# A fused attention and expert kernel: the first stage's loads four units ahead and in program order, TensorE's order left to the scheduler

## The chip, the cores and the metric

The kernel runs on one core of one Trainium2 chip. The metric is device time in microseconds (us) of one execution. A core has TensorE (PE, matrix multiplies into PSUM banks), VectorE (DVE), ScalarE (ACT), GpSimd (POOL) and SyncE (SP, which here issues every DMA). Each engine works through its own list of instructions, and that list is fixed when the program is built.

## The reference, cut to what matters

Three blocks follow one another on float32 data:

```
# 1  q, k, v: (4, 8 heads, 576, 64)
out_d     = softmax(q_d @ k_d.T / 8) @ v_d      # q_d, k_d, v_d: means over 4 positions (144 rows)
out_local = softmax(q @ k.T / 8, masked to |i - j| < 4) @ v
x = repeat(out_d, 4) + out_local                # -> (4, 576, 512)
# 2  a token mixer, then a channel mixer
u = x + (relu(x.T @ w_tok1) @ w_tok2).T         # w_tok1 576x256, w_tok2 256x576
x = u + relu(u @ w_ch1) @ w_ch2                 # w_ch1 512x1536, w_ch2 1536x512
# 3  four attention experts with causal masks, each row weighted by its two best gates
```

The weights of block 2 arrive in a 64-bit format and are turned into float32 on the core. They, and the activations that meet them, are split into a high and a low part, so that each product is three matmuls.

## The kernel before, in words

**Units.** The first stage (blocks 1 and the token mixer of 2) loops over 16 units, a batch `b` and a pair of heads `p` each. A unit's data are `qT` (queries, transposed), `kz` (keys, two halves in a zeroed tile), `vz` (values in windows of 64 positions, two halves in a zeroed tile) and `vp` (values for the mean). `load_qk` (L271) loads the first two and `load_v` (L254) the others. `load_v` also adds up `vp` into `vd` on GpSimd (L265, L266).

**Steps.** Step `i` of the loop at L468 does, in program order: `load_qk` of unit `i+3`; `values(i)` (matmuls into `pod` and `ol`, and the sum into `u`); `local(i+2)` and `pooled(i+2)` (scores `sl` and `sd`, `kd`, the maxima `nmx` and `nd`, the exponentials into `P` and `Pd`); `turns(i+1)` (transposes `tl` and `pdt`, copied to `PT` and `PdT` by ScalarE); `tok_step(i)`; four pieces of the token mixer's weights, while there are any; from step 3 on one piece `wc` of the channel mixer's weights, six in all for its first group; and `load_v` of unit `i+3`. `tok_step` (L461) does the token mixer for the pair of units whose last is done: transposes `tx` (`tok_turn`) and then the second product `pu` (`tok_second`) of an older pair in even steps, the first product `h` (`tok_first`) in odd steps.

**Weights.** `load_f32` (L166) loads a 64-bit piece into one of two `raw64` buffers, and ScalarE, VectorE and GpSimd convert it (L190 to L200); `split` then makes its two parts.

**Buffers.** `KB` (3) counts the `kz` and `qz` tiles, `VB` (3) the `vz` tiles and the units that `load_v` is ahead, `LA+1` (3) the units that `load_qk` is ahead. `qT` has 3 buffers, `vp` 2, `vd` 3. `pod`, `ol`, `sd`, `tl`, `tx`, `h` and `pu` share 4 PSUM banks; `sl` and `pdt` share 2 double ones.

**What sets the order.** The framework's scheduler simulates the program when it is built and gives each engine its list: an instruction is put in when the simulation has it ready, the earlier or the favoured one (`PRI`) first. VectorE's, ScalarE's, GpSimd's and SyncE's lists come from this. TensorE's list in the first stage is written out by hand: `behind` (L90) chains each matmul and transpose to the one before in program order, with

```
tc.add_manual_dep(ins.ins, order["last"].ins.name, ...NoSync..., reason="order")
```

SyncE's list isn't chained: a load is issued where the simulation found its buffer free.

After the stage, `order["on"] = False` (L487), and stage two (the channel mixer, L570 on) and the experts follow, whose order is the scheduler's.

Of the kernel before, what the change touches and what calls it, by code (L numbers as in the profile page):

```python
# [7 lines left out]
F32 = mybir.dt.float32  # L8
# [8 lines left out]
B, H, S, D = 4, 8, 576, 64  # L17
# [9 lines left out]
PK, PQ = SD // 2, 2 * SD // 3  # L27
# [18 lines left out]
ZENG = ['any', 'any']  # L46
PRE = False
ABANKS, CBANKS = (4, 2), (6, 1)
START = 'q0 q1 v0 q2 v1 v2'
XLO = 'gpsimd'  # L50
CONV0 = 3
UB = 5
TAIL = [1, 1, 1, 1]
ULO = 'vector'
LA = 2
WT = 4
VB = 3
KB = 3


@with_exitstack
def body(ctx, tc, qT, kT, vw, vp, wt1, wt2, wc1, wc2, wq, wk, wvg, wo, out):
    nc = tc.nc

    def pool(name, side=None, space=None, stack=ctx):
        kw = {"side": side} if side else {}
        if space is not None:
            kw["space"] = space
        return stack.enter_context(tc.tile_pool(name=name, bufs=1, reuse_waits="tile", **kw))
# [13 lines left out]
    def ahead(part):  # L83

        return tc.high_priority(offset=PRI[part]) if part in PRI else nullcontext()

    def spare(kind, i=0):

        return nc.vector if i < VEC.get(kind, 0) else nc.gpsimd

    order = {"on": True, "last": None}

    def behind(ins):

        if order["on"]:
            if order["last"] is not None:
                tc.add_manual_dep(ins.ins, order["last"].ins.name,
                                  mybir.DependencyInfo(mybir.DependencyClass.NoSync, mybir.DependencyReason.DATA),
                                  reason="order")
            order["last"] = ins  # L100

    def mm(*a, **kw):
        behind(nc.tensor.matmul(*a, **kw))  # L103

    def tp(*a):
        behind(nc.tensor.transpose(*a))
# [29 lines left out]
    def split(hi, lo, src, relu=False, scale=None):  # L136
        nc.scalar.activation(hi, src, AF.Relu if relu else AF.Copy, **({"scale": scale} if scale else {}))  # L137
        lowpart(lo, src, hi, relu, scale)
# [18 lines left out]
    def flat(t, shape):  # L157
        return t.rearrange("p c n -> p (c n)") if len(shape) == 3 else t

    def load_split(p, dram, shape, name, stage):  # L160
        raw = stage.tile(shape, F32, tag="raw", bufs=2, name=name + "_raw")
        nc.sync.dma_start(raw, dram)
        hi = p.tile(shape, F32R, name=name + "_hi")
        lo = p.tile(shape, F32R, name=name + "_lo")
        split(hi, lo, raw)
        return hi, lo  # L166

    def load_f32(dram, shape, name, dst=None):

        P0, n = shape[0], 1  # L170
        for d in shape[1:]:
            n *= d
        if dram.dtype == F32:
            if dst is None:
                dst = pv.tile(shape, F32, tag="w64t", bufs=2, name=name + "_t")
            nc.sync.dma_start(dst, dram)
            return dst
        raw = pv.tile([P0, n, 2], I32, tag="raw64", bufs=2, name=name + "_raw")
        d32 = dram.bitcast(I32)
        if len(shape) == 3:  # L180
            nc.sync.dma_start(raw.rearrange("p (c n) t -> p c (n t)", c=shape[1]), d32)
        else:
            nc.sync.dma_start(raw.rearrange("p n t -> p (n t)"), d32)
        h = raw[:, :, 1]
        a = pv.tile([P0, n], I32, tag="w64a", bufs=2, name=name + "_a")
        f = pv.tile([P0, n], I32, tag="w64f", bufs=2, name=name + "_f")
        g = pv.tile([P0, n], F32, tag="w64g", bufs=2, name=name + "_g")
        t = pv.tile([P0, n], F32, tag="w64t", bufs=2, name=name + "_t")

        nc.scalar.activation(t.bitcast(I32), raw.bitcast(U32)[:, :, 0], AF.Copy, scale=2.0 ** -29)  # L190

        nc.scalar.activation(g, h.bitcast(F32), AF.Abs)

        nc.vector.tensor_scalar(a, h, 3, 0x3FFFFFF8, op0=OP.logical_shift_left, op1=OP.bitwise_and)
        nc.vector.scalar_tensor_tensor(f, h, -0x40000000, a, op0=OP.bitwise_and, op1=OP.bitwise_or)
        nc.vector.scalar_tensor_tensor(f.bitcast(F32), g, 2.0 ** -15, f.bitcast(F32), op0=OP.is_ge, op1=OP.mult)
        if dst is None:
            dst = t.rearrange("p (c n) -> p c n", c=shape[1]) if len(shape) == 3 else t

        nc.gpsimd.tensor_tensor(flat(dst, shape).bitcast(I32), f, t.bitcast(I32), op=OP.add)  # L200
        return dst
# [12 lines left out]
    pa = pool("pa", stack=sA)  # L214
# [27 lines left out]

    KZ = [pa.tile([128, 2, S], F32, name=f"kz{i}") for i in range(KB)]
    VZ = [pa.tile([128, 2, NW, D], F32, name=f"vz{i}") for i in range(VB)]

    QZ = [pa.tile([128, 2, SD], F32, name=f"qz{i}") for i in range(KB)]

    def zero(tiles, i, eng):

        for h in range(2):  # L250
            eng.memset(tiles[i][64 * h:64 * h + 64, 1 - h], 0.0)

    Vl, Vd = {}, {}

    def load_v(b, p):
        i = b * NP + p
        if i < VB:
            zero(VZ, i, getattr(nc, ZENG[1]))
        Vl[b, p] = VZ[(b * NP + p) % VB]
        for h in range(2):  # L260
            nc.sync.dma_start(Vl[b, p][64 * h:64 * h + 64, h], vw[b, p, 64 * h:64 * h + 64])
        raw = pa.tile([PK, 4, 4, D], F32, tag="vp", bufs=2, name=f"vp{b}{p}")
        nc.sync.dma_start(raw, vp[b, p])
        vd = pa.tile([PK, 4, D], F32, tag="vd", bufs=3, name=f"vd{b}{p}")
        spare("v", i).tensor_tensor(raw[:, :, 0:2], raw[:, :, 0:2], raw[:, :, 2:4], op=OP.add)  # L265
        spare("w", i).tensor_tensor(vd, raw[:, :, 0], raw[:, :, 1], op=OP.add)  # L266
        Vd[b, p] = vd
# [1 line left out]
    QK = {}  # L269

    def load_qk(b, p):  # L271
        q = pa.tile([128, S], F32, tag="qT", bufs=3, name=f"qT{b}_{p}")
        nc.sync.dma_start(q, qT[b, p])
        i = b * NP + p
        if i < KB:
            zero(KZ, i, getattr(nc, ZENG[0]))
            zero(QZ, i, nc.gpsimd)
        kz = KZ[i % KB]
        for h in range(2):
            nc.sync.dma_start(kz[64 * h:64 * h + 64, h], kT[b, p, 64 * h:64 * h + 64])  # L280
        QK[b, p] = (q, kz, QZ[i % KB])

    SC = {}
# [82 lines left out]
    def values(b, p):  # L366
        PT, PdT = TR.pop((b, p))
        po = b1("pod")
        vd = Vd[b, p]
        for k in range(2):  # L370
            for h in range(2):
                mm(po[64 * h:64 * h + 64, :SD], vd[:, 2 * h + k], PdT[:, k, h * SD:(h + 1) * SD],
                                 start=k == 0, stop=k == 1)
        OdT = pa.tile([128, SD], F32, tag="OdT", bufs=2, name="OdT")
        nc.scalar.activation(OdT, po[:, :SD], AF.Copy)
        up = OdT[:, :, None].to_broadcast([128, SD, 4])
        for w0, w1 in ((0, 4), (4, NW)):
            o = b1("ol")
            s0 = w0 * WQ
            s1 = min(w1 * WQ, S)  # L380
            for w in range(w0, w1):
                q0 = w * WQ
                n = min(WQ, S - q0)
                r0 = 64 * (w % 2) + q0 - KS[w]
                for h in range(2):
                    mm(o[64 * h:64 * h + 64, q0 - s0:q0 - s0 + n], Vl[b, p][:, h, w],
                                     PT[:, w // 2, r0:r0 + n], start=True, stop=True)
            nc.vector.tensor_tensor(U[b][:, p, s0:s1].rearrange("p (g r) -> p g r", r=4),
                                    o[:, :s1 - s0].rearrange("p (g r) -> p g r", r=4),
                                    up[:, s0 // 4:s1 // 4], op=OP.add)  # L390
# [44 lines left out]
    units = [(b, p) for b in range(B) for p in range(NP)]  # L435
    for what in START.split():
        (load_qk if what[0] == "q" else load_v)(*units[int(what[1])])

    n = len(units)
# [20 lines left out]

    def tok_step(i):  # L461

        for what, k in ((tok_turn, i - 2), (tok_first, i - 3), (tok_second, i - 4)):
            if k % 2 == 0 and 0 <= k < n:
                with ahead(what.__name__):
                    what(units[k][0], units[k][1] // 2)

    for i in range(n):  # L468
        if i + LA + 1 < n:
            load_qk(*units[i + LA + 1])  # L470
        values(*units[i])
# [7 lines left out]
        tok_step(i)  # L479
        for _ in range(WT):  # L480
            if tokw:
                tokw.pop(0)()
        if i >= CONV0 and conv[0][0] == 0:
            convert()
        if i + VB < n:
            load_v(*units[i + VB])
    order["on"] = False  # L487
    sA.close()


# [279 lines left out]
    for i, (b, p) in enumerate(pairs):  # L770
# [13 lines left out]
        last = nxt is None  # L784
# [80 lines left out]
```

## Time and profile before

| | |
|---|---|
| time, median of 3 runs | 832.79 us (830.56 to 835.46) |
| time of the profiled execution | 831.15 us |
| its span, first to last instruction | 829.3 us |
| TensorE busy | 696.0 us, 84% of the span |
| VectorE, ScalarE, GpSimd busy | 492.0, 392.2, 163.4 us |
| mean granted TensorE clock | 0.925 of full speed |
| moved by DMA | 46.88 MB |

The profile's page shows the span in 40 slices of some 20.7 us. In the first thirteen, which hold the first stage, TensorE is busy for 4, 4, 2, 4, 4, 6, 8, 5, 6, 8, 5, 8 and 9 tenths, and after them for 9 or more in nearly all. VectorE's for the first six are 5, 5, 9, 8, 9 and 5. A row of the windows view gives, for one stretch, what each engine was busy; a row of the waits view, who waited for whom, in all, how often and at most; a row of the timeline, one instruction or a run of like ones, with the idle time before it and what ended that in brackets. "Busy" leaves out all time in which an engine stands at an instruction that isn't ready.

### The profile page before, as it was taken

Reading aid. Unit: us, or ns where it says so; the run is one execution under the profiler, and the core shown is the slowest. Engines: PE = TensorE matmul, PEld = TensorE weight load, DVE = VectorE, ACT = ScalarE, POOL = GpSimd, SP = SyncE. Lnnn points to the kernel's source line nnn. Section 1 sums busy time; section 2 is a strip of 40 time slices with the busy share of each in tenths; the row PEclk is TensorE's granted clock in tenths of the full one; section 3 lists DMA queues with packets and bytes.
Section 4 is the critical chain, followed back from the end, with each engine's and each line's share of the span. In section 5 each row is a group of like instructions: output and inputs, shape, how many; then the busy total and the mean of one; then the engine's idle time right before and its main releaser. Section 6 shows DMA issues by size and latency. Waiting matters only on the chain. (4 is left out here: it accounts for less than half of the span.)

```text
span 829.3 us, 15409 instructions
## 1 busy us (share of the span) xinstructions
PE 696.0 (84%) x5816; PEld 648.7 (78%) x5816; DVE 492.0 (59%) x1203; ACT 392.2 (47%) x1273; POOL 163.4 (20%) x183
## 2 busy tenths in 40 slices
PE   4424468568589999999999999999989989989994
PEld 3324368557578999999999999999987868779863
DVE  5598955334445479487558445644287556657760
ACT  6356653363365254354344223422266475566662
POOL 5575653333321012020011000000420010010000
PEclk8567598798799999999999999999999999999997
DMA  8545552252210022031011001000021031021111
GB/s 208 141 126 171 157 123 60 60 117 60 59 34 2 1 89 65 2 116 37 1 51 53 1 1 39 15 1 1 1 58 31 1 86 30 9 78 30 44 45 57
DMA packets 28578, 46.88 MB, mean 57 GB/s; under 512 B 3224, under 2 KB 16024, under 8 KB 28504
## 3 DMA queue, kind: packets, MB, share of 16 engines
q1 hardware_dynamic: 28504, 45.90, 20.7%
q8 instruction: 46, 0.75, 0.4%
q14 instruction: 28, 0.23, 0.1%
HBM read 36.45 MB, written 4.72 MB: 50 GB/s over the span
## 5 line engine op out<-in xcount | busy, mean ns | idle before, releaser
L103 PE MATMUL c<-ul,wch 128*128 128x288 f32 x384 | 113.7, 296 | 0.6 <-DVE ul L506 0.6
L103 PE MATMUL c<-uh,wch 128*128 128x288 f32 x384 | 113.6, 296 | 0.4 <-DVE acc L529 0.4
L103 PE MATMUL c<-hh,wch 128*128 128x288 f32 x384 | 113.8, 296 | 0.0
L103 PE MATMUL c<-hh,wcl 128*128 128x288 f32 x384 | 113.2, 295 | 0.0
L103 PE MATMUL c<-hl,wch 128*128 128x288 f32 x384 | 113.2, 295 | 0.0
L103 PE MATMUL c<-uh,wcl 128*128 128x288 f32 x384 | 113.2, 295 | 0.0
L137 ACT ACTIVATE hh<-c 128x288 fp32r<-128x288 f32 x96 | 39.1, 408 | 122.1 <-PE c L103 122.1
L143 DVE SCALAR_TENSOR_TENSOR hl<-c,hh 128x288 fp32r<-128x288 f32 x96 | 43.5, 453 | 64.6 <-ACT hh L137 64.6
L103 PEld LDWEIGHTS c<-ul,wch 128*128 128x128 f32 x384 | 72.4, 189 | 1.5 <-DVE ul L506 1.3
L103 PEld LDWEIGHTS c<-uh,wch 128*128 128x128 f32 x384 | 72.2, 188 | 0.9 <-DVE acc L529 0.9
L103 PEld LDWEIGHTS c<-hh,wch 128*128 128x128 f32 x384 | 72.2, 188 | 0.2
L103 PEld LDWEIGHTS c<-hl,wch 128*128 128x128 f32 x384 | 72.3, 188 | 0.0
L103 PEld LDWEIGHTS c<-hh,wcl 128*128 128x128 f32 x384 | 72.3, 188 | 0.0
L103 PEld LDWEIGHTS c<-uh,wcl 128*128 128x128 f32 x384 | 72.2, 188 | 0.0
L200 POOL TENSOR_TENSOR wc_t<-wc_f,wc_t 128x512 int32<-128x512 int32 x24 | 33.7, 1409 | 171.3 <-ACT wc_t L190 155.3
L505 ACT ACTIVATE uh<-u 128x288 fp32r<-128x288 f32 x128 | 52.9, 441 | 27.3 <-PE c L103 27.3
L506 DVE TENSOR_TENSOR ul<-u,uh 128x288 fp32r<-128x288 f32 x128 | 56.4, 470 | 8.8 <-ACT uh L505 8.7
L700 ACT ACTIVATE Pc<-s,nm 112x576 f32<-112x576 f32 (+4 forms) x80 | 44.3, 555 | 25.6 <-DVE nm L697 13.2
L103 PE MATMUL pod<-PdT,vd 72*64 72x144 f32 x128 | 13.4, 339 | 50.7 <-ACT PdT L363 45.7
L103 PE MATMUL pu<-wt_hi,h1h 128*128 128x288 f32 x64 | 24.0, 375 | 36.4 <-DVE xl L147 35.2
L319 ACT ACTIVATE P<-sl,nmx 128x64 f32<-128x64 f32 x160 | 48.6, 341 | 8.7 <-DVE nmx L313 8.6
L295 DVE TENSOR_REDUCE kd<-kz 128x144 f32<-128x1152 f32 x16 | 21.6, 1348 | 51.3 <-DMA kz<-in_kT_dram 51.3
(166 smaller groups left out, 1880.1 us busy)
## 6 DMA issues: line engine op xcount, KB each, us to landing
wc_raw<-in_wc_dram SPq DMA_DIRECT2D x24, 512.0 KB
vz<-in_vw_dram SPq DMA_DIRECT2D x32, 160.0 KB
qT<-in_qT_dram SPq DMA_DIRECT2D x16, 288.0 KB
kz<-in_kT_dram SPq DMA_DIRECT2D x32, 144.0 KB
vp<-in_vp_dram SPq DMA_DIRECT2D x16, 288.0 KB
K<-K SPq DMA_DIRECT2D x64, 72.0 KB
out_dram<-y SPq DMA_DIRECT2D x16, 232.0 KB
wt_raw<-in_wt_dram SPq DMA_DIRECT2D x4, 288.0 KB
```

The lines of the kernel that those rows point to most:

```text
L103: behind(nc.tensor.matmul(*a, **kw))
L137: nc.scalar.activation(hi, src, AF.Relu if relu else AF.Copy, **({"scale": scale} if scale else {}))
L143: nc.vector.scalar_tensor_tensor(lo, src, 0.0, h, op0=OP.max, op1=OP.subtract)
L200: nc.gpsimd.tensor_tensor(flat(dst, shape).bitcast(I32), f, t.bitcast(I32), op=OP.add)
L295: nc.vector.tensor_reduce(kd, kz.rearrange("p h (g r) -> p g h r", r=4), axis=AX.XY, op=OP.add)
L319: nc.scalar.activation(P[:, t, h], sv[:, bk, i], AF.Exp, bias=nmx[:, bk, i:i + 1], scale=0.125, accum_out=sm[:, t, h:h + 1])
L505: nc.scalar.activation(hi, u, AF.Copy)
L506: getattr(nc, ULO).tensor_tensor(lo, u, hi.bitcast(F32), op=OP.subtract)
L700: nc.scalar.activation(pv_, sv, AF.Exp, bias=nm[:nq], accum_out=su[:nq])
```

## The change

Seven things are changed, all but the last in the first stage.

1. Before the loop the loads go `q0 q1 v0 q2 v1 q3 v2 v3`, one unit more of each; in the loop `load_qk` is of unit `i+4` and `load_v` of `i+4`.
2. There are 4 tiles of `kz`, `qz`, `vz`, `qT` and `vd` instead of 3, and 3 of `vp` instead of 2.
3. All loads of the stage, the weights' too, go through `fetch`, which chains each to the one before: SyncE issues them in program order.
4. `order["on"]` is False: TensorE's list in the stage comes from the scheduler, as the other engines' lists do.
5. In `tok_step` the second product stands ahead of the transposes.
6. Three pieces of the token mixer's weights per step instead of four.
7. The memory that GpSimd's own DMA queue would use is cut to 1024 bytes, which makes room for the tiles.

```diff
-START = 'q0 q1 v0 q2 v1 v2'
+START = 'q0 q1 v0 q2 v1 q3 v2 v3'
-LA = 2
-WT = 4
-VB = 3
-KB = 3
+LA = 3
+WT = 3
+VB = 4
+KB = 4
-    order = {"on": True, "last": None}
+    order = {"on": False, "last": None}
+    queue = {"on": True, "last": None}
+
+    def fetch(dst, src):
+
+        ins = nc.sync.dma_start(dst, src)
+        if queue["on"]:
+            if queue["last"] is not None:
+                tc.add_manual_dep(ins.ins, queue["last"].ins.name,
+                                  mybir.DependencyInfo(mybir.DependencyClass.NoSync, mybir.DependencyReason.DATA),
+                                  reason="queue")
+            queue["last"] = ins
...
-            nc.sync.dma_start(Vl[b, p][64 * h:64 * h + 64, h], vw[b, p, 64 * h:64 * h + 64])
-        raw = pa.tile([PK, 4, 4, D], F32, tag="vp", bufs=2, name=f"vp{b}{p}")
-        nc.sync.dma_start(raw, vp[b, p])
-        vd = pa.tile([PK, 4, D], F32, tag="vd", bufs=3, name=f"vd{b}{p}")
+            fetch(Vl[b, p][64 * h:64 * h + 64, h], vw[b, p, 64 * h:64 * h + 64])
+        raw = pa.tile([PK, 4, 4, D], F32, tag="vp", bufs=3, name=f"vp{b}{p}")
+        fetch(raw, vp[b, p])
+        vd = pa.tile([PK, 4, D], F32, tag="vd", bufs=VB, name=f"vd{b}{p}")
...
-        q = pa.tile([128, S], F32, tag="qT", bufs=3, name=f"qT{b}_{p}")
-        nc.sync.dma_start(q, qT[b, p])
+        q = pa.tile([128, S], F32, tag="qT", bufs=KB, name=f"qT{b}_{p}")
+        fetch(q, qT[b, p])
...
-        for what, k in ((tok_turn, i - 2), (tok_first, i - 3), (tok_second, i - 4)):
+        for what, k in ((tok_second, i - 4), (tok_turn, i - 2), (tok_first, i - 3)):
...
-    order["on"] = False
+    order["on"] = queue["on"] = False
...
-    nc = bacc.Bacc("TRN2", target_bir_lowering=False, num_devices=1)
+    nc = bacc.Bacc("TRN2", target_bir_lowering=False, num_devices=1, dynamic_dma_scratch_size=1024)
```

The loads in `load_split`, `load_f32` and of `kz` are changed to `fetch` in the same way.

## Rows read from the trace of the kernel before

**Rows 1.** Windows: stretch, length, busy (x count) PE, PEld, DVE, ACT, POOL; clock, DMA share, GB/s.
```profile
0.00:35.28 35.28, 10.83 (x80) 8.37 (x80) 16.35 (x32) 17.62 (x67) 17.38 (x41) 0.72 0.71 185
35.28:98.00 62.72, 24.19 (x289) 21.76 (x289) 58.14 (x84) 34.94 (x123) 41.56 (x40) 0.66 0.53 155
98.00:131.86 33.86, 25.29 (x250) 23.95 (x250) 21.87 (x43) 16.68 (x78) 17.31 (x18) 0.76 0.36 88
...
163.10:194.08 30.98, 20.44 (x251) 19.27 (x250) 12.33 (x30) 13.02 (x64) 11.20 (x14) 0.83 0.36 79
...
225.00:248.63 23.63, 20.12 (x252) 19.12 (x251) 11.02 (x28) 12.92 (x64) 5.69 (x6) 0.93 0.10 30
248.63:266.25 17.62, 16.38 (x217) 15.53 (x216) 8.72 (x20) 8.97 (x38) 2.16 (x2) 1.00 0.00 1
```

**Rows 2.** Waits, 0 to 240 us: engine, line, releaser: total us, times, longest.
```profile
DVE kd L295 <- DMA kz<-in_kT_dram: 51.3, 11, 8.9
...
PE sl L103 <- DMA kz<-in_kT_dram: 0.6, 1, 0.6
```

**Rows 3.** Waits of SyncE's queue over the whole span.
```profile
SPq L263 <- POOL vd L266: 89.5, 10, 14.5
```

**Rows 4.** Timeline of one slow step, SyncE: start us, us, instruction.
```profile
180.68 1.10 SPq L280 DMA_DIRECT2D kz<-in_kT_dram  x2
```

**Rows 5.** Timeline of that step, VectorE.
```profile
186.97 1.35 DVE L295 TENSOR_REDUCE kd<-kz 128x144 f32<-128x1152 f32 x1 [8.47 <-DMA kz<-in_kT_dram]
188.25 1.61 DVE L147 TENSOR_TENSOR xl<-tx,xh 116x512 fp32r<-116x512 f32 x3
```

**Rows 6.** Timeline of that step, TensorE.
```profile
173.09 0.71 PE L103 MATMUL pod<-PdT,vd 72*64 72x144 f32 x8 [1.12 <-ACT PdT L363]
...
178.30 1.26 PE L106 MATMUL tx<-ident,u 128*116 128x128 f32 x10
188.98 0.61 PE L103 MATMUL pu<-wt_hi,h1h 128*128 128x288 f32 x1 [9.42 <-DVE xl L147]
...
194.08 0.71 PE L103 MATMUL pod<-PdT,vd 72*64 72x144 f32 x8
```

**Rows 7.** Waits, 225 to 248.63 us.
```profile
PE pu L103 <- DVE xl L147: 2.4, 1, 2.4
```

**Rows 8.** Groups of VectorE, 35.28 to 98 us: form, count, busy us, mean ns, idle.
```profile
L194 DVE TENSOR_SCALAR wc_a<-wc_raw 128x512 int32<-128x512 int32 x8 | 7.4, 923 | 2.1 <-DMA wc_raw<-in_wc_dram 2.0
L196 DVE SCALAR_TENSOR_TENSOR wc_f<-wc_g,wc_f 128x512 f32<-128x512 f32 x7 | 6.3, 900 | 0.4 <-ACT wc_g L192 0.3
L147 DVE TENSOR_TENSOR wcl<-wc_t,wch 128x512 fp32r<-128x512 f32 x6 | 5.8, 967 | 0.0
...
L195 DVE SCALAR_TENSOR_TENSOR wc_f<-wc_raw,wc_a 128x512 int32<-128x512 int32 x7 | 5.7, 808 | 0.2
```

**Rows 9.** Timeline of the start, SyncE.
```profile
14.42 2.08 SPq L181 DMA_DIRECT2D wt_raw<-in_wt_dram  x2
```

**Rows 10.** Timeline of the start, ScalarE.
```profile
28.41 0.67 ACT L190 ACTIVATE wt_t<-wt_raw 116x512 int32<-116x512 uint32 x1 [6.56 <-DMA wt_raw<-in_wt_dram]
...
29.55 0.76 ACT L357 ACTIVATE PT<-tl 128x384 f32<-128x384 f32 x2
33.47 0.67 ACT L190 ACTIVATE wt_t<-wt_raw 116x512 int32<-116x512 uint32 x1 [3.15 <-DMA wt_raw<-in_wt_dram]
```

**Rows 11.** Timeline of the start, TensorE: the first unit's values.
```profile
35.28 1.23 PE L103 MATMUL pod<-PdT,vd 72*64 72x144 f32 x8 [10.81 <-ACT PdT L363]
```

**Rows 12.** DMA issues of the page: tile, queue, count, KB each.
```profile
vz<-in_vw_dram SPq DMA_DIRECT2D x32, 160.0 KB
qT<-in_qT_dram SPq DMA_DIRECT2D x16, 288.0 KB
kz<-in_kT_dram SPq DMA_DIRECT2D x32, 144.0 KB
vp<-in_vp_dram SPq DMA_DIRECT2D x16, 288.0 KB
```

More of the change, by code (lines that the diff above doesn't have):

```diff
@@ L161, in load_split @@
         raw = stage.tile(shape, F32, tag="raw", bufs=2, name=name + "_raw")
-        nc.sync.dma_start(raw, dram)
+        fetch(raw, dram)
         hi = p.tile(shape, F32R, name=name + "_hi")
@@ L175, in load_f32 @@
                 dst = pv.tile(shape, F32, tag="w64t", bufs=2, name=name + "_t")
-            nc.sync.dma_start(dst, dram)
+            fetch(dst, dram)
             return dst
@@ L180, in load_f32 @@
         if len(shape) == 3:
-            nc.sync.dma_start(raw.rearrange("p (c n) t -> p c (n t)", c=shape[1]), d32)
+            fetch(raw.rearrange("p (c n) t -> p c (n t)", c=shape[1]), d32)
         else:
-            nc.sync.dma_start(raw.rearrange("p n t -> p (n t)"), d32)
+            fetch(raw.rearrange("p n t -> p (n t)"), d32)
         h = raw[:, :, 1]
@@ L279, in load_qk @@
         for h in range(2):
-            nc.sync.dma_start(kz[64 * h:64 * h + 64, h], kT[b, p, 64 * h:64 * h + 64])
+            fetch(kz[64 * h:64 * h + 64, h], kT[b, p, 64 * h:64 * h + 64])
         QK[b, p] = (q, kz, QZ[i % KB])
```

## The prediction

> **What bounds the kernel now.** I read the page's slices first: TensorE is busy for nine tenths or more behind the first stage and for half in it, so the change can pay only there. I then cut the stage at the first matmul of a unit's values (`pod`; v0 is unit 0's, of 16 in all) with the windows view. v0 stands at 35.28 us [rows 11], and the windows end at v3, v5, ..., v15 at 266.25 us [rows 1]; the pairs from v5 to v7, v7 to v9 and v9 to v11 are alike (one stands, 30.98 us). The reader is to see four things.
>
> *From v5 to v11 nothing is full.* In 30.98 us TensorE is busy for 20.44, ScalarE 13.02, VectorE 12.33, GpSimd 11.20, and the DMA engines for 0.36 [rows 1]. It is a chain of waits. The waits view gives its largest link: VectorE at `kd` for a transfer of `kz`, 51.3 us in 11 times [rows 2]. In the timeline of one such step SyncE issues `kz` at 180.68 to 181.78, VectorE stands 8.47 us and begins `kd` at 186.97, and only then `xl`, the low part of the transposes `tx`, at 188.25 [rows 4, 5]. TensorE, whose next instruction is `pu` behind `tx`, stands 9.42 us until 188.98, and the next values come at 194.08, 20.99 us after those at 173.09 [rows 6]. `kd` is needed two units later: it stands too early in VectorE's list.
>
> *The loop closes through SyncE.* It waits for a `vp` buffer until GpSimd has made a `vd`, 89.5 us in 10 times [rows 3], and `kz` is queued behind.
>
> *From v11 on the loads have landed*, and the same list of matmuls takes 23.63 us a pair, 7.35 less, with only 2.4 us at `pu` [rows 1, 7].
>
> *From v0 to v3 VectorE is full:* 58.14 of 62.72 us [rows 1], of which the channel mixer's weights, pulled in early, are 7.4 + 6.3 + 5.8 + 5.7 = 25.2 [rows 8]. v0 itself is late since ScalarE, in order, stands at `wt_t` until a weight lands, at 28.41 and at 33.47, with the copies to `PT` between the two; TensorE stands 10.81 us for `PdT` [rows 10, 11].
>
> **The change, part by part,** against the profiled execution's 831.15 us, which is 1.64 under the median of 832.79. (Every sum is given as a change of 831.15; 1.6 is added for the median.)
>
> *One unit more ahead of the loop, and the weights behind it.* The first weights were issued from 14.42 us [rows 9]. Now `q3`, `v3` and `q4` go out first where only `q3` did: a `q` is 288 + 2 x 144 = 576 KB, a `v` 2 x 160 + 288 = 608 KB [rows 12], so 1184 KB (1.21 MB) more, 6.6 us at the 185 GB/s of this stretch [rows 1]. If ScalarE's list keeps its order, v0 is 6.6 late; if it puts `PT` and `PdT` ahead of `wt_t`, the 10.81 us of [rows 11] go. Bounds +6.6 and -10.8; the row at hand is the first order, so I take +3.
>
> *Weights in program order.* A channel weight's load comes with step 3 and later, one a step. The 25.2 us leave VectorE between v0 and v3, which leaves 58.14 - 25.2 = 32.9 for three units. VectorE no longer sets the pace; the nearest row is the steady pace, 30.98 / 2 = 15.5 a unit, 46.5 for three: 46.5 - 62.72 = -16. Bounds 0 (another wait takes over) and 3 x 11.8 - 62.72 = -27 (the pace of v11 to v13). Three pieces of the token mixer's weights a step for four move one or two pieces a step on; their first user, `h` of step 3, comes after them, so nothing.
>
> *From v3 to v5,* 33.86 us with VectorE at 21.87: this pair holds both the stall and two of the new conversions. I take 27, -7, with bounds 0 and -10.2 (23.63).
>
> *From v5 to v11.* Three buffers of `vp` and four of `vd` take GpSimd out of the loop: the `vp` of unit i+4 waits for a `vd` made a step ago. `pu` ahead of `tx`, and a list that may place it anywhere, take the 9.42 us wait of TensorE for `xl` away, as `pu` reads nothing that `kd` holds up. What is late next is `xh` and `xl` themselves, as between v11 and v13. I take 25 a pair: 23.63, and half of the two `kd` (2.7 us) that those pairs lack. That is 3 x (25 - 31) = -18. Four conversions now fall here, each some 3.6 us of VectorE (0.923 + 0.900 + 0.967 + 0.808 [rows 8]); VectorE has 31 - 12.3 us idle, so I count 1 us each, +4 (bounds 0 and 14, uncovered). Sum -14, bounds -22 and 0.
>
> A rule on the queue weighs against this. The row shows SyncE standing 89.5 us at a `vp` with `kz` behind it [rows 3]. The Trainium skill, DMA: Bandwidth & Descriptors, "Anatomy of one DMA", says that a DMA's semaphore wait is spent on the issuing sequencer before dispatch; the trace agrees. By that rule a load chained behind a waiting one isn't ahead at all, and the sum would be that of rival B.
>
> *From v11 on* the loads were in anyway. TensorE's free list may fill the 2.4 us at `pu` [rows 7] and the like of 1.12 at `pod` [rows 6], 3.5 a pair; for two pairs half of that, -3 (bounds -7 and +3).
>
> *At nothing:* zeroing the fourth tiles (it lies in the first microseconds, under the first loads; at most 1 us uncovered). The issues are as many as before. Every DMA is SyncE's, as these [rows 12], and none GpSimd's, so its smaller queue costs nothing. Stage two has TensorE full in either case; conversions that were done early and now fall there are covered by a VectorE half idle.
>
> Sum: +3 - 16 - 7 - 14 - 3 = -37. 831.15 - 37 = 794, and 796 for the median.
>
> **The rivals.**
>
> *A, TensorE becomes the bound.* Depth and a free list together take all waits: pairs from v3 on at the 20.1 us that TensorE was busy between v11 and v13 [rows 1], six of them 121 us for 168.25, -48; v0 to v3 at 11.8 a unit, -27; v0 as it is. -75: 756, 758 for the median (745 with v0's wait gone). For it: no engine but VectorE in one stretch is full. Against it: the pairs without a load wait still took 23.63, by chains from unit to unit (exponentials, copies) that the change leaves.
>
> *B, the stall stays.* `kz` of unit i+5 is chained behind `vz` of unit i+4, which waits for values(i); it leaves when it did before. If the build again puts `kd` into VectorE's list at the time that it thinks `kz` lands, depth buys nothing: the consumer moves up with the load. For it: `kd` of a unit stood two units ahead of its use and waited all the same [rows 2, 5]. Against it: `pu` no longer hangs on it. Price: the pairs gain only 2 each, -6, and lose 4 to conversions; -3 for v3 to v5; -16; and v0 at its bad end, +6.6. -14: 817, 818 for the median.
>
> *C, slower: TensorE now stands for loads.* Its hand-written list takes a `kz` only where program order puts it, and it waited 0.6 us for one in the whole stage [rows 2]. A list from the simulation puts scores wherever it thinks that the data are in, as VectorE's list did, at 51.3 / 11 = 4.7 us a time [rows 2]. At each of the 12 units from the fifth on this is 56 us against the 37 gained: +19, 850 (852 for the median). It decides from 37 / 12 = 3.1 us a unit. Against it: scores need one of two double PSUM banks, shared with `pdt`, so they can't run far ahead.
>
> *D, nothing happens:* the waits change places, the loads arrive earlier and are used when they were. About 831 (833). Against it: the conversions move for certain.
>
> **How the numbers follow.** A measurement can tell 0.5% from no change, so "same" is 829 to 837. The forecast (775 to 812) 0.48; A 0.15; B (812 to 828) 0.20; D 0.06; C 0.11. Faster is forecast, A and B, 0.83; same is D, 0.06; slower is C, 0.11. The range takes in B and most of A, and the bounds of v0 and of the conversions: 752 to 830. Outside lie C, part of D and A's lower end, about 0.2.
>
> **What would show it.** Right: v15 near 230 us instead of 266; no conversion of a channel weight before v3 and v0 to v3 under 50 us; pairs of 25 us from v5 on, and no wait of `pu` for `xl` above 3 us; SyncE no longer waiting for `vd`. VectorE's wait for `kz` under 20 us in the stage speaks for the forecast or A; above 40 us for B. C shows as waits of `sl` for `kz` or `qT` on TensorE of over 3 us a unit. The prediction is wrong if v0 comes after 45 us, if units 3 to 8, which now carry a conversion each, take over 17 us a unit, or if the second stage grows by more than 5 us.

## The result, and the profile after

The changed kernel takes 785.16 us (781.57 to 788.42) beside 831.99: ratio 0.943, 95% interval 0.938 to 0.948. The forecast was 796, in a range of 752 to 830. The profiled execution spans 784.1 us. The time lies in the range, 11 us under the forecast; several terms of the sum stand for the wrong cause, which only the experiments show.

The windows view of the changed kernel, cut as in [rows 1] at the first `pod` of v0, v3, v5, v9, v11, v13 and v15, with v5 to v9 left out (columns: stretch, length, busy time of PE, PEld, DVE, ACT, POOL; clock, DMA share, GB/s):

```profile
0.00:43.83 43.83, 13.11 (x108) 11.09 (x110) 20.30 (x39) 20.39 (x72) 26.07 (x51) 0.73 0.59 152
43.83:75.21 31.38, 22.20 (x292) 19.92 (x290) 17.99 (x48) 22.24 (x106) 14.98 (x19) 0.83 0.71 168
75.21:104.58 29.37, 22.68 (x251) 20.41 (x250) 22.45 (x45) 18.37 (x74) 20.16 (x23) 0.88 0.50 124
...
160.14:185.54 25.40, 23.04 (x250) 20.90 (x251) 15.05 (x36) 13.49 (x64) 12.20 (x13) 0.87 0.37 97
185.54:207.04 21.50, 20.82 (x249) 19.34 (x251) 13.18 (x32) 12.95 (x64) 8.44 (x10) 0.92 0.10 31
207.04:222.12 15.08, 15.08 (x195) 14.31 (x191) 7.55 (x20) 8.64 (x37) 2.16 (x2) 1.00 0.01 2
```

Read the lengths against those of before: v0 is 8.5 us later, v0 to v3 takes half, the pairs after it are shorter, and in the last two windows TensorE is all but full. In TensorE's column the work is the same; what went is time between. From v15 on both kernels take as long (562 and 563 us).

Whole-stage waits of the changed kernel, 0 to 240 us (who waited for whom: total, times, longest), and then SyncE's own:

```profile
POOL vp L277 <- DMA vp<-in_vp_dram: 42.4, 13, 7.5
DVE kd L307 <- DMA kz<-in_kT_dram: 39.7, 14, 4.7
...
PE pdt L118 <- POOL Pd L357: 14.9, 4, 11.8
...
PE tl L118 <- POOL P L336: 12.0, 1, 12.0
```

```profile
SPq L106 <- PE ol L115: 89.2, 10, 13.4
```

VectorE still waits for `kz`, 39.7 us for 51.3 [rows 2]. SyncE still waits as long, for the values' matmuls (`ol`) instead of for `vd` [rows 3]: the chain of loads now hangs on the `vz` tile. But no wait of `pu` for `xl` is left among TensorE's, and its two longest lie before v0.

### The profile page after: what moved, and what is told of

Read it like the earlier page. It is cut to its first block, busy times and chain, and to the rows that moved or that the text cites. A ratio compares the mean times of both kernels' runs of the same rounds, so it can differ in the third digit from the quotient of the medians.

```text
span 784.1 us, 15356 instructions
## 1 busy us (share of the span) xinstructions
PE 697.3 (89%) x5816; PEld 647.4 (83%) x5816; DVE 478.1 (61%) x1205; ACT 395.4 (50%) x1275; POOL 158.9 (20%) x185
## 5 line engine op out<-in xcount | busy, mean ns | idle before, releaser
L331 ACT ACTIVATE P<-sl,nmx 128x64 f32<-128x64 f32 x160 | 47.5, 329 | 16.7 <-DVE nmx L325 14.9
L307 DVE TENSOR_REDUCE kd<-kz 128x144 f32<-128x1152 f32 x16 | 21.6, 1349 | 39.7 <-DMA kz<-in_kT_dram 39.7
L709 DVE TENSOR_REDUCE nm<-s 112x1 f32<-112x576 f32 (+4 forms) x80 | 40.5, 514 | 8.5 <-PE s L705 7.4
L621 POOL TENSOR_TENSOR vlo<-u,vh 128x576 fp32r<-128x576 f32 x16 | 22.6, 1443 | 91.4 <-ACT vh L620 91.4
```

The costliest lines, as they stand in the source:

```text
L307: nc.vector.tensor_reduce(kd, kz.rearrange("p h (g r) -> p g h r", r=4), axis=AX.XY, op=OP.add)
L331: nc.scalar.activation(P[:, t, h], sv[:, bk, i], AF.Exp, bias=nmx[:, bk, i:i + 1], scale=0.125, accum_out=sm[:, t, h:h + 1])
L621: getattr(nc, XLO).tensor_tensor(lo, U[b][:, c], hi.bitcast(F32), op=OP.subtract)
L709: nc.vector.tensor_reduce(nm[:nq], sv, axis=AX.X if t < 4 else AX.XY, op=OP.max, negate=True)
```

## The experiments

Each kernel ran beside the kernel before on the same chip, and ratios are to that. Parts of the first stage, in us, from the first `pod` of each unit in the timeline:

| kernel | median | ratio (95%) | v0 at | v0-v3 | v3-v5 | v5-v11 | v11-v15 | v15 at |
|---|---|---|---|---|---|---|---|---|
| before | 831.99 | 1 | 35.3 | 62.7 | 33.9 | 93.1 | 41.2 | 266.2 |
| changed | 785.16 | 0.943 (0.938-0.948) | 43.8 | 31.4 | 29.4 | 81.0 | 36.6 | 222.1 |
| free_order_only | 797.09 | 0.959 (0.956-0.961) | 47.5 | 34.8 | 39.0 | 75.9 | 36.3 | 233.6 |
| written_order | 800.12 | 0.962 (0.959-0.965) | 29.2 | 53.4 | 28.4 | 86.0 | 42.5 | 239.5 |
| written_order_old_step | 816.11 | 0.982 (0.980-0.985) | 28.1 | 54.2 | 33.3 | 95.1 | 41.3 | 252.1 |
| old_step | 790.73 | 0.952 (0.948-0.955) | 44.8 | 30.9 | 31.5 | 83.1 | 36.4 | 226.7 |
| no_queue | 789.12 | 0.949 (0.947-0.952) | 48.5 | 39.7 | 34.6 | 63.7 | 33.8 | 220.3 |
| three_ahead | 782.73 | 0.941 (0.939-0.944) | 43.0 | 34.5 | 24.5 | 80.0 | 38.8 | 220.8 |
| three_ahead_no_queue | 789.68 | 0.948 (0.945-0.952) | 49.0 | 35.7 | 34.3 | 70.5 | 38.8 | 228.4 |
| weights_later | 782.35 | 0.940 (0.936-0.944) | 35.9 | 35.6 | 31.7 | 78.9 | 34.5 | 216.5 |
| kd_late | 776.77 | 0.935 (0.933-0.938) | 46.1 | 28.7 | 25.8 | 79.2 | 35.1 | 214.9 |
| kd_late_weights_later | 787.82 | 0.948 (0.946-0.951) | 36.7 | 36.4 | 33.5 | 82.2 | 36.0 | 224.7 |
| three_ahead_kd_late | 783.15 | 0.942 (0.939-0.945) | 38.0 | 30.0 | 27.2 | 81.8 | 38.8 | 215.8 |
| three_ahead_kd_vp_late | 779.50 | 0.937 (0.935-0.940) | 40.8 | 29.3 | 25.8 | 84.0 | 35.5 | 215.3 |

### TensorE's list alone: free_order_only

```diff
--- before
-    order = {"on": True, "last": None}
+    order = {"on": False, "last": None}
```

> The kernel before with one edit: TensorE's list in the first stage is left to the scheduler. Theory ORDER (the steady part gains because TensorE's list no longer stands behind VectorE's early kd): pairs of units from v5 to v11 fall from 31.0 to some 27 us and v11 to v15 from 41.3 to some 37, while v0 to v3 stays near 62: 812 to 818 us. Theory DEPTH (the gain is the extra unit of look-ahead): the pairs stay at 31, 828 to 836 us. Theory WEIGHTS (v0 to v3 gains because the channel mixer's weights are kept out of it by the chain of loads) says only that v0 to v3 stays above 55 us here, with eight conversions in it.

797 us: faster than any theory had it. The pairs from v5 to v11 fall to 25.3 us (75.9 / 3), under the 27 that ORDER named. v0 to v3 takes 34.8 us, where WEIGHTS wanted 55 or more with eight conversions in it. But only three of the eight are done there now and a fourth is begun, as v0 is late and the list another; the rest, and two more, make v3 to v5 longer, 39.0 us. None is left for v5 to v11. Up to v5 (121.4 us, for 131.9 before and 104.6 in the changed kernel) the other parts of the change still have their share. One line gives 34 of the 47 us.

### All but TensorE's list: written_order

```diff
--- changed
-    order = {"on": False, "last": None}
+    order = {"on": True, "last": None}
```

> The changed kernel with TensorE's list chained in program order again (the second product still ahead of the transposes in a step). ORDER: pairs from v5 to v11 at 29 to 31 us, v11 to v15 at 40 or more, v0 to v3 still near 32 to 45: 798 to 812 us. DEPTH: pairs as in the changed kernel, 27 us, 783 to 792 us. WEIGHTS alone: v0 to v3 under 45 us whatever the pairs do.

800 us, as ORDER had it, with pairs of 28.7, just under its 29. All parts but the free list are worth 32 us here, nearly as much as the free list alone. Against both ORDER and WEIGHTS, v0 to v3 is 53.4, neither near 32 nor under 45, though only one channel weight is begun there, at 79.98 us, 2.7 us before v3. VectorE is busy for 30.9 of the 53.4 us; TensorE's largest wait in this stretch is at `pod`, for ScalarE's copy `PdT`, 17.5 us where the kernel before had 36.2:

```profile
PE pod L115 <- ACT PdT L375: 17.5, 3, 10.6
```

v0 itself is at 29.2. VectorE's list has changed with TensorE's: it has unit 0's `rd`, the small reciprocal that scales `Pd`, at 23.27 us, ahead of the first conversion of a weight (`wt_a`, 32.03 us).

```profile
23.27 0.16 DVE L355 TENSOR_SCALAR rd<-sdm 96x3 f32<-96x3 f32 x1
```

As v0 starts so early, its time and that of v0 to v3 are better read together: v3 is at 82.7 us here and at 82.3 in free_order_only, for 98.0 before and 75.2 in the changed kernel.

### The place of the second product: written_order_old_step and old_step

```diff
--- written_order (old_step: the same edit on the changed kernel)
-        for what, k in ((tok_second, i - 4), (tok_turn, i - 2), (tok_first, i - 3)):
+        for what, k in ((tok_turn, i - 2), (tok_first, i - 3), (tok_second, i - 4)):
```

> The changed kernel with TensorE's list chained in program order and the second product back behind the transposes: all that is left of the change is the loads (depth, chain, three pieces). Beside written_order (800 us) it tells what the second product's place is worth in a chained list. By the mechanism that the prediction named (TensorE stands at pu for xl, 9.4 us a pair): pairs from v5 to v11 back to 30 or 31 us, with waits of pu for xl of 25 us or more in all, 806 to 815 us. Rival (the loop through SyncE was what made that wait, and it is gone): within 4 us of 800.

> The changed kernel with the second product back behind the transposes in program order; TensorE's list stays free. If a free list makes the place in the program idle (the scheduler puts pu where it is ready): within 4 us of the changed kernel's 785. If program order still decides through the priorities: pu late again, pairs from v5 to v11 at 29 or more, 793 to 801 us, as much as the place was worth in a chained list.

In a chained list the place is worth 16 us (816 for 800, a little more than was expected) and the pairs go back to 31.7, as before the change or slightly over. The wait of `pu` for `xl` is back as well, but smaller than was expected (13.6 us in 4, not 25). In the stretch from v5 to v11 TensorE's larger wait is for the same transposes:

```profile
PE tx L118 <- ACT PT L369: 15.4, 2, 7.9
```

So in the chained list, whatever stands behind `tx` pays for what holds `tx` up. In a free list (old_step) it is 791 against 785, between the two expectations: a third of those 16 us, with intervals that just touch, so that its size is uncertain.

written_order_old_step is also the loads alone: depth, chain and three weight pieces a step, with none of the order. They are worth 2%, all of it before v5: from v5 on 95.1 and 41.3 us, where the kernel before has 93.1 and 41.2.

### The chain of loads and the depth: no_queue, three_ahead, three_ahead_no_queue

```diff
--- changed: no_queue
-    queue = {"on": True, "last": None}
+    queue = {"on": False, "last": None}
--- changed: three_ahead (three_ahead_no_queue: with the line above as well)
-START = 'q0 q1 v0 q2 v1 q3 v2 v3'
-LA = 3
-VB = 4
-KB = 4
+START = 'q0 q1 v0 q2 v1 v2'
+LA = 2
+VB = 3
+KB = 3
-        raw = pa.tile([PK, 4, 4, D], F32, tag="vp", bufs=3, name=f"vp{b}{p}")
+        raw = pa.tile([PK, 4, 4, D], F32, tag="vp", bufs=2, name=f"vp{b}{p}")
```

> The changed kernel with the chain of loads switched off; depth and free list of TensorE stay. WEIGHTS: channel weights are loaded and converted ahead of v3 again, v0 to v3 goes back to 50 to 62 us, v0 comes earlier (35 to 40 instead of 43.8): 800 to 812 us. DEPTH and ORDER, without WEIGHTS: within 4 us of the changed kernel's 785.

> The changed kernel with the depth of before: three units ahead, three tiles of kz, qz, vz, qT and vd and two of vp; the chain of loads, the free list of TensorE and the three weight pieces a step stay. DEPTH: most of the steady gain goes, pairs from v5 to v11 back to 30 us or more: 797 to 810 us. ORDER and WEIGHTS: loads are used as soon as the build thinks they land, whatever the depth; within 5 us of 785, and v0 some 4 us earlier, as 1.2 MB less stands ahead of the first weights.

> The kernel before with TensorE's list free, the second product first in a step and three weight pieces a step: no depth, no chain of loads. Free list alone gave 797 us, with the chain at this depth 783. If the chain of loads is worth the difference: 793 to 800 us. If the second product's place is, and the chain is worth nothing: 782 to 787 us.

three_ahead: 783 us. The fourth unit of look-ahead is worth nothing here, and DEPTH is out; the pairs are at 26.7, not 30. v0, expected 4 us earlier, came 0.8 earlier. With or without the chain, a depth of three or four gives the same within the intervals (782.7 and 785.2; 789.7 and 789.1).

no_queue: 789, within the 4 us of DEPTH and ORDER, against the 800 or more of WEIGHTS. v0 to v3 takes 39.7 us, not 50 or more, and v0 comes 4.7 us later, where WEIGHTS had it earlier. v0 to v5 is longer than in the changed kernel by 13.5 us, but v5 to v11 takes 63.7 us instead of 81.0, and v15 is at 220.3 for 222.1. The windows of no_queue show why:

```profile
48.55:88.20 39.65, 27.17 (x292) 23.65 (x291) 36.18 (x63) 26.58 (x113) 30.38 (x32) 0.72 0.58 168
88.20:122.80 34.60, 22.74 (x254) 19.92 (x250) 30.33 (x53) 22.72 (x81) 23.44 (x20) 0.90 0.64 171
122.80:186.50 63.70, 61.24 (x756) 55.35 (x757) 46.24 (x100) 43.06 (x213) 32.76 (x39) 0.97 0.37 93
```

Nine of the ten channel weights that the stage converts are begun before v5 here, three in the changed kernel. So VectorE is nearly full in the first stretch (36.18 of 39.65) and TensorE in the last (61.24 of 63.70). The chain moves the conversions; they have to be done somewhere, and the stage's end hardly notices. What the chain is worth at last is 4 us at a depth of four (intervals overlap) and 7 at three, where they just do not.

three_ahead_no_queue (790) lies between its two expectations. From free_order_only (797) to it, the second product's place and the three weight pieces are worth 7 us; the chain gives 7 more (783).

### The late first unit: weights_later

```diff
--- changed
-        for _ in range(WT):
+        for _ in range(WT if i else 0):
```

> The changed kernel with the token mixer's weights loaded from step 1 on instead of step 0, so that none is queued or converted before the first unit's values. Theory HEAD (VectorE and ScalarE stand, in order, for the first weights, which holds up Pd and PdT of unit 0 and costs the end of the stage as much): v0 at 27 to 32 instead of 43.8 us, v15 8 to 12 us earlier, 773 to 779 us. Rival SHIFT (the conversions are work that has to be done somewhere, and the units behind pay for them): v0 early as well, but v0 to v3 longer by the same, v15 within 4 us of 222: 782 to 788 us.

The changed kernel's start, VectorE, then GpSimd, then TensorE in the timeline:

```profile
36.36 0.43 DVE L206 TENSOR_SCALAR wt_a<-wt_raw 116x512 int32<-116x512 int32 x1 [3.98 <-DMA wt_raw<-in_wt_dram]
36.70 0.16 DVE L355 TENSOR_SCALAR rd<-sdm 96x3 f32<-96x3 f32 x1
...
37.73 3.13 POOL L357 TENSOR_TENSOR Pd<-Pd,rd 96x432 f32<-96x432 f32 x2 [3.60 <-DVE rd L355]
...
40.05 1.17 PE L118 MATMUL pdt<-ident,Pd 96*72 96x96 f32 x6 [11.79 <-POOL Pd L357]
```

A small reciprocal chain (`rd`) stands behind a conversion whose weight has not landed; GpSimd and TensorE wait in turn. Taking the weights away brings v0 to 35.9 (HEAD wanted 27 to 32), and v0 to v3 then takes 4.2 us more: the first weights are waited for there now, 8.1 us by VectorE, and TensorE stands 7.8 us at `pod` for `PdT`. 782 us, with an interval that overlaps the changed kernel's: of the 8 us gained at v0 half is paid back at once, between HEAD and SHIFT.

### The early kd: kd_late, and it with other edits

```diff
--- changed: kd_late
+    hold = {"last": None}
-        nc.vector.tensor_reduce(kd, ...)
+        red = nc.vector.tensor_reduce(kd, ...)
+        if hold["last"] is not None:
+            tc.add_manual_dep(red.ins, hold["last"].ins.name, ...NoSync..., reason="hold")
...
-        nc.vector.tensor_scalar_mul(nmx, nmx, 0.125)
+        hold["last"] = nc.vector.tensor_scalar_mul(nmx, nmx, 0.125)
--- three_ahead_kd_late: three_ahead with this; kd_late_weights_later: weights_later with this
--- three_ahead_kd_vp_late: three_ahead_kd_late, three vp tiles, the sums of vp moved behind P
-        spare("v", i).tensor_tensor(raw[:, :, 0:2], raw[:, :, 0:2], raw[:, :, 2:4], op=OP.add)
-        spare("w", i).tensor_tensor(vd, raw[:, :, 0], raw[:, :, 1], op=OP.add)
+        Vd[b, p] = (vd, raw)
+    def sum_v(b, p, after):          # called in local(), behind the scaling of P
+        vd, raw = Vd[b, p]
+        first = nc.gpsimd.tensor_tensor(raw[:, :, 0:2], raw[:, :, 0:2], raw[:, :, 2:4], op=OP.add)
+        tc.add_manual_dep(first.ins, after.ins.name, ...NoSync..., reason="sum")
+        nc.gpsimd.tensor_tensor(vd, raw[:, :, 0], raw[:, :, 1], op=OP.add)
+        Vd[b, p] = vd
```

> The changed kernel with one order more: kd of a unit may not stand in VectorE's list before the maxima nmx of the unit before it. VectorE's wait for kz, 39.7 us in 14 times in the changed kernel, falls below 10. Theory STALL (that wait still delays the rest of VectorE's list): v5 to v11 from 81 to 65 to 72 us, 770 to 778 us. Rival COVERED (with TensorE's list free, VectorE stands there while nothing else of its list is due): within 4 us of 785, or slower if kd now comes too late for sd, up to 795.

> Both orders together: kd behind the nmx of the unit before, and the token mixer's weights from step 1 on. kd_late alone gave 777 us, the weights alone 782. If they remove different waits: v0 near 36 instead of 46 and v15 at 208 to 211, 769 to 774 us. If the work of the weights only shifts to the next units: 775 to 779 us.

> kd behind the nmx of the unit before, at the depth of before (three units ahead, chain of loads, free list). If depth is worth nothing even where kd no longer stands early: within 4 us of kd_late's 777. If the wait for kz was what hid the worth of depth: 783 to 795 us, as kz now has one unit less to land in.

> As the one before, with GpSimd's sums of vp taken out of load_v: they stand behind the scaling of P of the same unit, and vp has three tiles. GpSimd's wait for vp, 42 us in the changed kernel, falls below 15. If that wait delays P and Pd behind it: 5 to 10 us under three_ahead_kd_late. If GpSimd stands there while nothing else of its list is due, or the sums come too late for pod: within 4 us of it, or slower.

kd_late is the fastest kernel here, 777 us, and its interval (up to 0.9375) stays just below the changed kernel's (from 0.9378). VectorE's wait for `kz` is all but gone (0.4 us), and the first rows of its waits are now:

```profile
DVE wt_a L206 <- DMA wt_raw<-in_wt_dram: 21.0, 4, 13.5
DVE h1l L155 <- ACT h1h L149: 9.5, 5, 2.9
```

But it did not do so in the way that STALL had it: v5 to v11 is 79.2 us, not 65 to 72. Of 40 us of waiting taken away, 8 came out at the end, spread over all parts behind v0. The wait of `wt_a` for its weight grew from 9.2 to 21.0 us; the rest was covered, as COVERED has it, though that is argued from the small gain and not shown by itself.

Nor does the gain add up. With the weights later as well the kernel takes 788, slower than with either edit; both theories had it under 780. At a depth of three kd_late is worth nothing (783.2 for 782.7). Put the other way, with `kd` held back the fourth unit of depth is worth 6 us (776.8 for 783.2), and these intervals do not overlap. That is the second of the two expectations for three_ahead_kd_late: depth may be worth something once `kd` no longer stands early. It stays open, as each edit gives the scheduler another start and the lists come out differently; the kernels with a free list lie between 777 and 797 us, and differences of 5 us among them are not told apart by a mechanism here.

three_ahead_kd_vp_late takes 779.5, 4 under three_ahead_kd_late, with intervals that touch: no clear gain, as its second expectation had it. GpSimd's wait for `vp` is gone, as expected, and the waits of that engine begin with:

```profile
POOL pool L310 <- DMA qT<-in_qT_dram: 38.1, 11, 8.0
```

In three_ahead_kd_late its wait for `vp` was 30.7 us and that for `qT` 1.5. The wait has moved to the next load in the list.

## Why the prediction was right, and which of its steps were not

| term | forecast | bounds | measured |
|---|---|---|---|
| v0 | +3 | -10.8 to +6.6 | +8.5 |
| v0 to v3 | -16 | -27 to 0 | -31.3 |
| v3 to v5 | -7 | -10.2 to 0 | -4.5 |
| v5 to v11 | -14 | -22 to 0 | -12.2 |
| v11 to v15 | -3 | -7 to +3 | -4.7 |
| rest | 0 | | -1.1 |
| span | -37 | | -45.2 |

Of the signs that were named, an early v15 (222 us), no channel weight converted before v3 (the first is begun at 78.95 us), no wait of `pu` for `xl` and none of SyncE for `vd` came. The pairs of 25 us from v5 on did not (27.0 in the mean), nor a wait for `kz` under 20.

**The start.** Outside its bounds, by 2 us, and from another part of the change. The step priced the loads; with the same loads and the written list v0 is at 29.2, toward the good end, and with the free list and the old loads at 47.5. ScalarE kept its order and stood for the weights, as the bad end had it; what the step missed is that, with TensorE's list free, VectorE's list puts `rd` behind a weight's conversion, and `Pd` waits for it (the rows under weights_later).

**v0 to v3.** Right in sign, beyond its bound, and half of the cause. The prediction said that the conversions leave, that VectorE no longer sets the pace, and that three units then take 46.5 us. They do leave, and VectorE is then busy for 30.9 us, near the 32.9 of the step; but with the written list the three units take 53.4, a third of the gain, and only with the free list on top 31.4. Part of that split is the start's: in the changed kernel v0 is late and three of the seven conversions of the token mixer's weights are begun before it, in written_order none. At v3 the loads alone give 15.7 us of the 22.8 (82.3 in written_order_old_step), where the two steps together had forecast 13; the free list alone gives the same 15.7, and both do not add up. And what the conversions leave here they bring back later: no_queue, which does them early, needs 13.5 us more from v0 to v5 and 17.3 less from v5 to v11. The step on v5 to v11 priced that at 4, for four conversions. Ten are done in the stage, the six that its loop asks for and four of the code behind it: three from v3 to v5 and seven from v5 to v11.

**v5 to v11.** The size was right (-12.2 for -14) and one of two causes, so part of that agreement is luck. "Three buffers of vp and four of vd take GpSimd out of the loop" is false as a gain: the loads alone leave this stretch at 95.1 us. SyncE's wait went from `vd` to `ol`, the same 89 us, as the rule on the queue and rival B had it. "pu ahead of tx, and a list that may place it anywhere" is what carries it: the place gives 95.1 to 86.0, the free list 86.0 to 81.0. The free list alone, without either, gives 75.9, with none of the ten conversions in this stretch.

**Rival B was half right**, and the sign that was named for it shows it. VectorE's wait for `kz` is 39.7 us, just under the 40 above which it should have spoken for B and far from the 20 of the forecast; only its price is not paid, since TensorE no longer stands behind it. That wait and the time had come apart, which the prediction's test did not foresee. **A** did not come: TensorE is busy for 138 of the first 200 us. **C** did not either: TensorE's wait of `sl` for `kz` is 1.3 us in the stage. Its free list stands elsewhere, at unit 0.

The step that failed by name is the one on depth, that more buffers of `vp` and `vd` take GpSimd out of the loop: alone the loads leave v5 to v11 at 95.1 us. With it fail the start, which priced the loads and left out what the free list does to VectorE's list, and the pace of v0 to v3, which took 46.5 us for what is 53.4 without the free list. The ladder that the runs give is: loads 831 to 816, the second product's place to 800, the free list to 785; from the other end, the free list alone 831 to 797, the second product's place and the three pieces to 790, the chain to 783, depth to 785. Parts that remove the same wait do not add. What stays open is why, among lists that are equally free, one is 10 us better than another (kd_late beside kd_late_weights_later).

## What to carry to other kernels

A wait for a transfer can be an order, not a lateness: while the consumer stood two units ahead of its use in an in-order list, one more buffer bought nothing here (785 with four, 783 with three). Ask who stands behind the waiting instruction, and free that engine first: here one line gave 34 us by itself, of 47 for the whole, though the other parts without it gave 32. Undo the parts one by one before crediting any, and check a named sign by its cost: here 40 us of waiting was worth 8.

## What the runs showed of the hardware

The same conversion on VectorE took very different times. `wt_f` of 116x512 (two SBUF inputs) took 1816 ns in the mean of the kernel before, twice, and 668 in the changed one. The rows, first of the kernel before, 35.28 to 98 us, then of the changed one, 0 to 222 us (line, form, count, busy us, mean ns, idle):

```profile
L196 DVE SCALAR_TENSOR_TENSOR wt_f<-wt_g,wt_f 116x512 f32<-116x512 f32 x2 | 3.6, 1816 | 0.0
```

```profile
L208 DVE SCALAR_TENSOR_TENSOR wt_f<-wt_g,wt_f 116x512 f32<-116x512 f32 x2 | 1.3, 668 | 0.0
```

In the kernel before, the second of them (37.48 to 39.46 us) lies beside GpSimd's work, which runs without a gap from 34.19 to 44.18. In the changed kernel GpSimd was busy beside the two as well (they lie at 37.77 to 39.03 us), and there its own instruction was the long one: the first of two `Pd` of one shape took 2264 ns, the other 898.

```profile
L357 POOL TENSOR_TENSOR Pd<-Pd,rd x2: 898/1581/2264, 37.7 to 40.0; 96x432 f32<-96x432 f32 x2
```

So one of the two engines may have stood for the other, VectorE in the kernel before and GpSimd in the changed one. That fits the Trainium skill, SBUF — State Buffer, "SBUF: two separate sides": the port pair that VectorE and GpSimd share is held by one of them for a whole instruction. No run here kept all else equal, so this is a reading, not shown. If it holds, VectorE's busy time from v0 to v3 [rows 1] held time in which it waited inside its instructions. What is measured is that the four-operation conversion priced at 3.6 us [rows 8] was 2.8 in the changed kernel from v3 to v11 (449 + 851 + 687 + 839 ns).
